# Attention and a two-layer network in one kernel: the first two pairs' k exponentials, the first decode blocks and constant products at the start

## The chip, the cores and the metric

One core of a Trainium2 chip runs the whole program. The metric is the device time of one execution in microseconds, the median of three runs. The trace is of one further execution of the same program.

## The reference

Shapes: batch 8, 8 heads, 576 tokens, head size 64, 128 features; 4608 tokens of 512 values go into a network of 512 to 2048 to 512.

```python
def phi(x):
    proj = np.einsum('bhsd,df->bhsf', x, w_phi)
    proj = proj - np.max(np.abs(proj), axis=-1, keepdims=True)
    return np.concatenate([np.exp(proj), np.exp(-proj)], axis=-1)
q_p, k_p = phi(q), phi(k)
kv = np.einsum('bhsf,bhsd->bhfd', k_p, v)
z = np.sum(k_p, axis=2)
num = np.einsum('bhsf,bhfd->bhsd', q_p, kv)
den = np.einsum('bhsf,bhf->bhs', q_p, z)[..., None] + 1e-06
attn = num / den                      # then heads side by side: x
h = x @ w_in
g = np.maximum(h, 0.0) + alpha * np.minimum(h, 0.0)
return g @ w_out
```

So exp(p - m) and exp(-(p - m)) = exp(-p + m) are wanted for every projected row p, where m is the largest absolute value of the row.

## The kernel before

Attention runs over 32 pairs of heads. A pair's k and q are one DMA (raw), laid with the head size on the partitions, so that one tile of 128 tokens of one head is the weights of a product with w_sb (w_phi), and 128 tokens x 128 features come out in PSUM. project(0) makes the first four tiles of k for both heads (16 product instructions in the trace); project(1) makes the last 64 tokens of k with 64 of q (the two small tiles pl), and then four tiles of q per head. VectorE takes the maximum m of the absolute values (L311) and subtracts it from the PSUM into a tile t in SBUF (L312). k_exp reads t on ScalarE, twice, with scale 1 and -1 (L325, and L320 for the last 64 tokens). q's t is turned by TensorE (q_turn) and its exponentials are taken from PSUM (L402, L404). k_z and k_acc sum and multiply with v on TensorE into the tile kv; kv_out copies it, kv_turn turns it, kv_copy copies it again; num and den are q's products with it.

PSUM: project(0) of the pairs 0 and 1 has a tile of its own per head, from the pool psf (two buffers, tag f); all other projections use one tile pj of both heads (ps_pj, one buffer). So each projection has to wait until the one before it has been read.

The weights of the network come as 64-bit numbers and are decoded in blocks of 256 columns, seven stages each: load (SP), scale (ScalarE), split (four VectorE instructions, L181 to L184), add (GpSimd), high (ScalarE), low (GpSimd), store (SP). Four buffers hold raw blocks.

The order is written out by hand: each step has a due time in units of a pair's slot (places, decode_at), all are sorted, and the engines PE, SP, DVE (VectorE) and Activation (ScalarE) keep that order. GpSimd's order, and the order of all engines in the second pass of the network behind this part, come from the planner of the framework. Pair i has project(0) at i - 0.9955, project(1) at i, k_exp(0) at i - 0.26, k_exp(1) at i + 0.0011, k_z at i + 1.0002, k_acc at i + 1.0012, the turns of kv and q from i + 1.1 on, den at i + 2.0004, num at i + 2.005. Decode block n of the first 20 has its split at 1 + n // 2 + 0.004 for even n and + 0.5 for odd n; its load is due 0.70 earlier, its scale 0.25 earlier, add, high and low 0.15, 0.42 and 0.55 later. "Project i/c" below means project(c) of pair i.

Of the kernel before, what the change touches and what calls it, by code (L numbers as in the profile page):

```python
# [8 lines left out]
F32 = mybir.dt.float32  # L9
F32R = mybir.dt.float32r  # L10
U32 = mybir.dt.uint32
AF = mybir.ActivationFunctionType
ALU = mybir.AluOpType
# [3 lines left out]
P = 128  # L17
B, H, S, D = 8, 8, 576, 64
FD = 128
# [20 lines left out]
WA = (0.0040, 0.50)  # L40
# [3 lines left out]
G_BUFS = 2  # L44
P_BUFS = 2
NV = 5
X_BUFS = 2
RAW_BUFS = 2
N2A = 3
# [59 lines left out]
def fused_kernel(ctx: ExitStack, tc: tile.TileContext, kq, v, w_phi, w_in, w_out, alpha, out):  # L109
# [24 lines left out]
    al = cst.tile([P, NF], F32, name="al")  # L134
# [1 line left out]
    act.dma_start(w_sb, w_phi)  # L136
    act.dma_start(al, alpha)
    aln = cst.tile([P, NF], F32, name="aln")
    dve.tensor_scalar(aln, al, -1.0, None, op0=ALU.mult)

    w1t = ctx.enter_context(tc.tile_pool(name="w1t", bufs=1, side="right"))
    ffn1 = ExitStack()
# [78 lines left out]
    def decode_at(t, blk):  # L221
        return [(t + (WT if t < TL else WL)[k], lambda u=u: u(*blk, WN)) for k, u in stages.items()]
# [38 lines left out]
    ps_pj = att.enter_context(tc.tile_pool(name="ps_pj", bufs=1, space=PSUM))  # L261
    ps_kv = att.enter_context(tc.tile_pool(name="ps_kv", bufs=1, space=PSUM))

    ones = cat.tile([P, 32], F32, name="ones")
    pool.memset(ones, 1.0)
    k4buf = []
# [5 lines left out]
    def attention_units(i):  # L272
        b, hp = divmod(i, NP)
        c = {}
# [8 lines left out]
            nc.sync.dma_start(c["v"], v[i])  # L283

        def project(ch):
            t = c["t", ch] = wk.tile([P, 2, 4 + ch, FD], F32, tag=f"t{ch}", name=f"t{i}_{ch}", bufs=1 + ch)
            dst, out, js = {}, [], [0, 1, 2, 3]
            if ch:
                js = [4] + js
                for h in range(2):  # L290
                    p1 = ps_m.tile([P, 1, 1, FD], F32, tag="m", name=f"pl{i}_{h}")
                    dst[h, 4] = p1[:, 0, 0]
                    out.append((slice(h, h + 1), slice(4, 5), p1))
            if ch == 0 and i < 2:
                for h in range(2):
                    p1 = psf.tile([P, 1, 4, FD], F32, tag="f", name=f"pj{i}_{ch}_{h}")
                    dst.update({(h, j): p1[:, 0, j] for j in range(4)})
                    out.append((slice(h, h + 1), slice(0, 4), p1))
            else:
                p2 = ps_pj.tile([P, 2, 4, FD], F32, tag="pj", name=f"pj{i}_{ch}")  # L300
                dst.update({(h, j): p2[:, h, j] for h in range(2) for j in range(4)})
                out.append((slice(0, 2), slice(0, 4), p2))
            for j in js:
                for h in range(2):
                    hs = slice(h * D, (h + 1) * D)
                    ts = slice((4 * ch + j) * P, (4 * ch + j + 1) * P)
                    pe.matmul(dst[h, j], lhsT=c["raw"][hs, ts], rhs=w_sb[hs], start=True, stop=True)  # L307
            for n, (hs, js, src) in enumerate(out):
                nh, nj = hs.stop - hs.start, js.stop - js.start
                m = wk.tile([P, nh, nj], F32, tag="m", name=f"m{i}_{ch}_{n}", bufs=4)  # L310
                dve.tensor_reduce(m, src, axis=AX.X, op=ALU.max, apply_absolute_value=True)  # L311
                dve.tensor_tensor(  # L312
                    t[:, hs, js], src, m.unsqueeze(3).broadcast_to([P, nh, nj, FD]), op=ALU.subtract
                )

        def k_exp(ch):
            if ch == 1:
                x = k4buf[i % 2]
                for a, sg in enumerate((1.0, -1.0)):
                    act.activation(x[0:64, a], c["t", 1][0:64, :, 0, :], AF.Exp, scale=sg)  # L320
                c["x", ch] = x.rearrange("p a (h n) f -> p a h n f", n=1)
                return
            x = wk.tile([P, 2, 2, 4, FD], F32, tag="x", name=f"xk{i}", bufs=X_BUFS)
            for a, sg in enumerate((1.0, -1.0)):
                act.activation(x[:, a], c["t", 0], AF.Exp, scale=sg)  # L325
            c["x", ch] = x

# [255 lines left out]
    def first_x():  # L583
        st = {}

        def fetch0():
            st["xr"] = xhl.tile([P, NK, C2], F32, tag="xr", name="xr2_0", bufs=XR_BUFS)
            nc.sync.dma_start(st["xr"], x_d[:, :, :C2].rearrange("k p s -> p k s"))
            xs[0] = []

        def cast0(j):
            if j % 2 == 0:
                st["xq"] = qp.tile([P, 2, 2, S], F32R, tag="qf", name=f"x2hl0{j}", bufs=QH_BUFS)
            xh, xl = (st["xq"][:, n, j % 2, :C2] for n in range(2))
            rnd(act, xh, st["xr"][:, j])
            xs[0].append((xh, xl))

        def low0(j):
            xh, xl = xs[0][j]
            low(dve, xl, st["xr"][:, j], xh)  # L600

        us = [(X0T[0], fetch0)]
        for j in range(NK):
            us.append((X0T[1 + j], lambda j=j: cast0(j)))
            us.append((X0T[1 + j] + X0L, lambda j=j: low0(j)))
        return us
# [10 lines left out]
    late += [(ff, z) for z in (1, 0) for ff in range(NF1 + NA, NF - NL)]  # L617
    blocks = [(ff, z, o) for ff, z in late for o in range(0, 512, WN)]
    for n, blk in enumerate(first):
        todo += decode_at(1 + n // 2 + WA[n % 2], blk)  # L620
    for n, blk in enumerate(blocks):
        todo += decode_at(W2A + W2D * n, blk)
    todo += first_x()
    et = mybir.EngineType
    pinned = {et.PE, et.SP, et.DVE, et.Activation}

# [174 lines left out]
```

## Time and profile before

| | us |
|---|---|
| median of 3 runs (1139.42 to 1140.46) | 1140.08 |
| the profiled execution's own time | 1140.04 |
| its span, first to last instruction | 1138.2 |
| PE busy | 1114.4 |
| DVE busy | 634.0 |
| ACT busy | 561.1 |
| POOL busy | 213.9 |

Busy time is summed over the instructions of an engine. Where rows carry a time in us from the start of the span, that is the start of the first instruction of the row, and the second number is the stretch that the row's instructions cover together. PE is TensorE, DVE VectorE, ACT ScalarE, POOL GpSimd, SP the engine that issues most DMAs.

### The profile page before, as it was taken

How to read it: one execution, taken by the hardware profiler on the slowest of the kernel's cores; microseconds unless marked ns; L12 is line 12 of the kernel's file. 1: busy time of each engine (PE TensorE's matmuls, PEld its weight loads, DVE VectorE, ACT ScalarE, POOL GpSimd, SP SyncE). 2: the span in 40 equal slices, each digit the busy share in tenths (PEclk: the TensorE clock that was granted, in tenths of full speed). 3: DMA queues.
4: the chain of work that ended last, by engine and by line, in shares of the span. 5: the costliest groups of instructions: out<-in, count | busy, mean ns of one | idle time of the engine just before them, and what ended most of it. 6: DMA issues, size and time to landing. Idle time of an engine off the chain costs nothing.

```text
span 1138.2 us, 18351 instructions
## 1 busy us (share of the span) xinstructions
PE 1114.4 (98%) x7232; PEld 865.2 (76%) x7232; DVE 634.0 (56%) x978; ACT 561.1 (49%) x1149; POOL 213.9 (19%) x219
## 2 busy tenths in 40 slices
PE   6999999999999999999999999999999999999998
PEld 5766767777777777677778788888888888888886
DVE  7888957798687777836861342424242333333322
ACT  4777656666666765664543333333333333433332
POOL 1345332322424142243542000000000000000000
PEclk9999999999999999999999999999999999999999
DMA  5467264555556365466627030303030302112021
GB/s 190 147 186 219 68 194 143 172 164 183 162 167 195 99 211 167 146 202 219 227 65 246 32 111 1 111 1 111 1 111 1 111 1 75 37 33 79 1 74 37
DMA packets 74101, 133.68 MB, mean 117 GB/s; under 512 B 14624, under 2 KB 24480, under 8 KB 73376
## 3 DMA queue, kind: packets, MB, share of 16 engines
q1 hardware_dynamic: 71712, 122.48, 33.7%
q0 software_dynamic: 2016, 9.96, 2.5%
q8 instruction: 57, 0.93, 0.3%
q14 instruction: 28, 0.23, 0.1%
q10 hardware_dynamic: 288, 0.07, 0.0%
HBM read 93.92 MB, written 38.42 MB: 116 GB/s over the span
## 4 chain that ended last, share of the span: by engine, by line
PE 88%; DVE 6%; DMA 4%; ACT 2%; issue 1%; SPq 0%; DVEq 0%; ACTq 0%
PE h L503 11%; PE h L505 11%; PE h L504 11%; PE po L511 8%; PE po L509 8%; PE po L510 8%; PE kv L348 6%; PE n L413 5%; PE pj L307 5%; PE o L511 3%; PE o L509 3%; PE o L510 3%; PE d L431 2%; PE qt L394 2%; DMA xr<-x_d 2%; PE kv L365 1%
## 5 line engine op out<-in xcount | busy, mean ns | idle before, releaser
L240 DVE SCALAR_TENSOR_TENSOR g<-r,aln,g 128x512 f32<-128x512 f32 x144 | 111.7, 775 | 307.1 <-ACT g L236 306.9
L235 ACT ACTIVATE r<-h 128x512 f32<-128x512 f32 x144 | 86.5, 601 | 293.3 <-PE h L505 293.2
L127 DVE TENSOR_TENSOR gl<-g,gh 128x512 fp32r<-128x512 f32 x144 | 104.7, 727 | 67.6 <-ACT gh L123 67.1
L123 ACT CAST gh<-g 128x512 fp32r<-128x512 f32 x144 | 90.0, 625 | 85.6 <-DVE g L240 85.6
L236 ACT ACTIVATE g<-h 128x512 f32<-128x512 f32 x144 | 86.0, 598 | 1.0 <-DMA part_d<-os 1.0
L509 PE MATMUL po<-gh,wd 128*128 128x512 f32 x216 | 84.6, 392 | 0.7 <-ACT gh L123 0.7
L510 PE MATMUL po<-gh,wd 128*128 128x512 f32 x216 | 84.7, 392 | 0.0
L511 PE MATMUL po<-gl,wd 128*128 128x512 f32 x216 | 84.5, 391 | 0.0
L311 DVE TENSOR_REDUCE m<-pj 128x8 f32<-128x1024 f32 (+1 forms) x66 | 78.2, 1185 | 10.4 <-PE pj L307 10.3
L307 PE MATMUL pj<-w_sb,raw 64*128 64x128 f32 x1024 | 73.2, 283 | 9.8 <-DMA w_sb<-w_phi_dram 4.6
L307 PEld LDWEIGHTS pj<-w_sb,raw 64*128 64x128 f32 x1024 | 64.1, 192 | 23.3 <-issue 15.6
L189 POOL TENSOR_TENSOR aw<-ew,aw 128x256 f32<-128x256 f32 x64 | 56.6, 885 | 128.6 <-DVE ew L184 128.6
L312 DVE TENSOR_TENSOR t<-pj,m 128x1024 f32<-128x1024 f32 (+1 forms) x66 | 78.7, 1192 | 2.3
L509 PE MATMUL o<-gh,w 128*128 128x512 f32 x180 | 76.0, 422 | 2.6 <-ACT os L554 2.4
L463 POOL TENSOR_TENSOR s<-s,rr 128x576 f32<-128x576 f32 x32 | 48.5, 1517 | 145.3 <-DMA rr<-rec_d 127.7
L503 PE MATMUL h<-xh,w 128*128 128x512 f32 x180 | 75.8, 421 | 0.0
L511 PE MATMUL o<-gl,w 128*128 128x512 f32 x180 | 71.7, 399 | 3.6 <-DVE gl L127 3.4
L404 ACT ACTIVATE qf<-qt 128x512 f32<-128x512 f32 x128 | 68.4, 615 | 6.3 <-PE qt L394 6.3
L511 PE MATMUL po<-gl,w 128*128 128x512 f32 x180 | 69.7, 390 | 1.4 <-DVE gl L127 1.4
L505 PE MATMUL h<-xl,w 128*128 128x512 f32 x180 | 70.7, 393 | 0.0
L510 PE MATMUL o<-gh,w 128*128 128x512 f32 x180 | 70.6, 392 | 0.0
L504 PE MATMUL h<-xh,w 128*128 128x512 f32 x180 | 70.5, 392 | 0.0
(105 smaller groups left out, 2402.6 us busy)
## 6 DMA issues: line engine op xcount, KB each, us to landing
xr<-x_d SPq DMA_DIRECT2D x18, 1024.0 KB
raw<-kq_dram SPq DMA_DIRECT2D x31, 576.0 KB
v<-v_dram SPq DMA_DIRECT2D x32, 320.0 KB
w_d<-raww SPq DMA_DIRECT2D x38, 256.0 KB
rr<-rec_d SPq DMA_DIRECT2D x64, 144.0 KB
x_d<-s SPq DMA_DIRECT2D x32, 288.0 KB
part_d<-os SPq DMA_DIRECT2D x36, 256.0 KB
pt<-part_d SPq DMA_DIRECT2D x9, 1024.0 KB
```

Source lines behind the costliest of these rows:

```text
L123: return act.copy(dst, src)
L127: return eng.tensor_tensor(dst, src, f(hi), op=ALU.subtract)
L235: act.activation(st["r"], ps, AF.Relu, scale=-1.0)
L236: act.activation(st["g"], ps, AF.Relu)
L240: dve.scalar_tensor_tensor(g, st["r"], aln[:, ff : ff + 1], g, op0=ALU.mult, op1=ALU.add)
L307: pe.matmul(dst[h, j], lhsT=c["raw"][hs, ts], rhs=w_sb[hs], start=True, stop=True)
L503: pe.matmul(ps, lhsT=wt[0][:, ws], rhs=xh, start=n == 0, stop=False)
L504: pe.matmul(ps, lhsT=wt[1][:, ws], rhs=xh, start=False, stop=False)
L505: pe.matmul(ps, lhsT=wt[0][:, ws], rhs=xl, start=False, stop=n == NK - 1)
L509: pe.matmul(ps, lhsT=wt[2][:, ws], rhs=gh, start=first, stop=False)
L510: pe.matmul(ps, lhsT=wt[3][:, ws], rhs=gh, start=False, stop=False)
L511: pe.matmul(ps, lhsT=wt[2][:, ws], rhs=gl, start=False, stop=last)
```

## The change

Four edits, all at the start of the kernel:

- Pairs 0 and 1 (i < NX): project(0) no longer subtracts the maximum on VectorE and has no tile t. VectorE makes the negative of the maximum in a small tile mn; ScalarE takes the exponentials from PSUM, one instruction per head, sign and tile of 128 tokens (16 per pair), with mn or m as bias.
- Decode blocks 0 and 1 have their splits due at 2.25 and 2.75 instead of 1.004 and 1.5; all their other stages move with them.
- A tile of ones (warm), set by VectorE, is multiplied by itself seven times (NWARM) into the PSUM tile that kv uses later, ahead of all other products; one exponential of it goes to ScalarE.
- The negative of alpha (aln) is made at due time 1.5 instead of first of all on VectorE.

```diff
@@ -44,6 +44,8 @@
 G_BUFS = 2
 P_BUFS = 2
 NV = 5
+NX = 2
+NWARM = 7
 X_BUFS = 2
 RAW_BUFS = 2
 N2A = 3
@@ -136,7 +138,6 @@
     act.dma_start(w_sb, w_phi)
     act.dma_start(al, alpha)
     aln = cst.tile([P, NF], F32, name="aln")
-    dve.tensor_scalar(aln, al, -1.0, None, op0=ALU.mult)
 
     w1t = ctx.enter_context(tc.tile_pool(name="w1t", bufs=1, side="right"))
     ffn1 = ExitStack()
@@ -261,6 +262,14 @@
     ps_pj = att.enter_context(tc.tile_pool(name="ps_pj", bufs=1, space=PSUM))
     ps_kv = att.enter_context(tc.tile_pool(name="ps_kv", bufs=1, space=PSUM))
 
+    warm = cat.tile([P, P], F32, name="warm")
+    dve.memset(warm, 1.0)
+    warm_e = cat.tile([P, 1], F32, name="warm_e")
+    act.activation(warm_e, warm[:, 0:1], AF.Exp)
+    ps_w = ps_kv.tile([P, 3, FD], F32, tag="kv", name="warm_up")
+    for n in range(NWARM):
+        pe.matmul(ps_w[:, 0], lhsT=warm, rhs=warm, start=True, stop=True)
+
     ones = cat.tile([P, 32], F32, name="ones")
     pool.memset(ones, 1.0)
     k4buf = []
@@ -283,7 +292,8 @@
             nc.sync.dma_start(c["v"], v[i])
 
         def project(ch):
-            t = c["t", ch] = wk.tile([P, 2, 4 + ch, FD], F32, tag=f"t{ch}", name=f"t{i}_{ch}", bufs=1 + ch)
+            if ch or i >= NX:
+                t = c["t", ch] = wk.tile([P, 2, 4 + ch, FD], F32, tag=f"t{ch}", name=f"t{i}_{ch}", bufs=1 + ch)
             dst, out, js = {}, [], [0, 1, 2, 3]
             if ch:
                 js = [4] + js
@@ -291,7 +301,7 @@
                     p1 = ps_m.tile([P, 1, 1, FD], F32, tag="m", name=f"pl{i}_{h}")
                     dst[h, 4] = p1[:, 0, 0]
                     out.append((slice(h, h + 1), slice(4, 5), p1))
-            if ch == 0 and i < 2:
+            if ch == 0 and i < NX:
                 for h in range(2):
                     p1 = psf.tile([P, 1, 4, FD], F32, tag="f", name=f"pj{i}_{ch}_{h}")
                     dst.update({(h, j): p1[:, 0, j] for j in range(4)})
@@ -309,6 +319,11 @@
                 nh, nj = hs.stop - hs.start, js.stop - js.start
                 m = wk.tile([P, nh, nj], F32, tag="m", name=f"m{i}_{ch}_{n}", bufs=4)
                 dve.tensor_reduce(m, src, axis=AX.X, op=ALU.max, apply_absolute_value=True)
+                if ch == 0 and i < NX:
+                    mn = wk.tile([P, nh, nj], F32, tag="mn", name=f"mn{i}_{n}", bufs=4)
+                    dve.tensor_scalar(mn, m, -1.0, None, op0=ALU.mult)
+                    c["pm", hs.start] = src[:, 0], m, mn
+                    continue
                 dve.tensor_tensor(
                     t[:, hs, js], src, m.unsqueeze(3).broadcast_to([P, nh, nj, FD]), op=ALU.subtract
                 )
@@ -321,7 +336,12 @@
                 c["x", ch] = x.rearrange("p a (h n) f -> p a h n f", n=1)
                 return
             x = wk.tile([P, 2, 2, 4, FD], F32, tag="x", name=f"xk{i}", bufs=X_BUFS)
-            for a, sg in enumerate((1.0, -1.0)):
+            for h in range(2) if i < NX else ():
+                src, m, mn = c["pm", h]
+                for a, (sg, bias) in enumerate(((1.0, mn), (-1.0, m))):
+                    for j in range(4):
+                        act.activation(x[:, a, h, j], src[:, j], AF.Exp, scale=sg, bias=bias[:, 0, j : j + 1])
+            for a, sg in enumerate((1.0, -1.0) if i >= NX else ()):
                 act.activation(x[:, a], c["t", 0], AF.Exp, scale=sg)
             c["x", ch] = x
 
@@ -617,10 +637,11 @@
     late += [(ff, z) for z in (1, 0) for ff in range(NF1 + NA, NF - NL)]
     blocks = [(ff, z, o) for ff, z in late for o in range(0, 512, WN)]
     for n, blk in enumerate(first):
-        todo += decode_at(1 + n // 2 + WA[n % 2], blk)
+        todo += decode_at(2.25 + 0.5 * n if n < 2 else 1 + n // 2 + WA[n % 2], blk)
     for n, blk in enumerate(blocks):
         todo += decode_at(W2A + W2D * n, blk)
     todo += first_x()
+    todo.append((1.5, lambda: dve.tensor_scalar(aln, al, -1.0, None, op0=ALU.mult)))
     et = mybir.EngineType
     pinned = {et.PE, et.SP, et.DVE, et.Activation}
 
```

## Rows read from the trace of the kernel before

**Rows 1.** The page's busy time, share of the span and instructions of each engine.
```profile
PE 1114.4 (98%) x7232; PEld 865.2 (76%) x7232; DVE 634.0 (56%) x978; ACT 561.1 (49%) x1149; POOL 213.9 (19%) x219
```

**Rows 2.** Busy time by stretch: stretch, length, each engine's busy us, granted clock, DMA.
```profile
0.00:10.00 10.00, 4.66 (x45) 4.50 (x47) 3.38 (x8) 1.82 (x2) 1.75 (x9) 1.00 0.51 166
10.00:20.00 10.00, 6.51 (x107) 5.02 (x104) 9.61 (x17) 5.46 (x10) 0.00 (x0) 1.00 0.83 279
20.00:30.00 10.00, 9.40 (x135) 6.88 (x133) 9.28 (x19) 7.52 (x18) 3.39 (x5) 1.00 0.37 127
30.00:40.00 10.00, 10.00 (x141) 7.12 (x137) 8.55 (x16) 8.14 (x19) 2.46 (x4) 1.00 0.08 26
```

**Rows 3.** TensorE's waits in 0 to 60 us: total, times, longest.
```profile
PE pj L307 <- DVE t L312: 3.5, 3, 2.1
```

**Rows 4.** Order of time, w_sb's load and TensorE's projections: start, us, instruction, idle before.
```profile
0.75 0.41 ACTq L136 DMA_DIRECT2D w_sb<-w_phi_dram  x1
...
4.57 2.08 PE L307 MATMUL pj<-w_sb,raw 64*128 64x128 f32 x16 [4.57 <-DMA w_sb<-w_phi_dram]
...
9.57 1.02 PE L307 MATMUL pj<-w_sb,raw 64*128 64x128 f32 x13 [0.77 <-DVE t L312]
...
19.12 1.16 PE L307 MATMUL pj<-w_sb,raw 64*128 64x128 f32 x16 [1.41 <-issue]
...
22.91 1.16 PE L307 MATMUL pj<-w_sb,raw 64*128 64x128 f32 x16 [0.60 <-DVE t L312]
...
28.51 1.16 PE L307 MATMUL pj<-w_sb,raw 64*128 64x128 f32 x16
...
39.09 1.16 PE L307 MATMUL pj<-w_sb,raw 64*128 64x128 f32 x16
```

**Rows 5.** Line 307 on TensorE in two stretches: ns least/median/most, first and last start.
```profile
L307 PE MATMUL pj<-w_sb,raw x10: 417/417/419, 4.9 to 5.8; 64*128 64x128 f32 x10
...
L307 PE MATMUL pj<-w_sb,raw x4: 271/272/272, 8.3 to 8.5; 64*128 64x128 f32 x4
```

**Rows 6.** Order of time, VectorE from 6 to 23 us, eight of its instructions.
```profile
6.69 0.69 DVE L311 TENSOR_REDUCE m<-pj 128x4 f32<-128x512 f32 x1 [1.09 <-PE pj L307]
...
9.34 0.28 DVE L311 TENSOR_REDUCE m<-pl 128x1 f32<-128x128 f32 x1
...
11.64 1.22 DVE L312 TENSOR_TENSOR t<-pj,m 128x1024 f32<-128x1024 f32 x1
12.78 0.68 DVE L311 TENSOR_REDUCE m<-pj 128x4 f32<-128x512 f32 x1
...
17.79 1.22 DVE L312 TENSOR_TENSOR t<-pj,m 128x1024 f32<-128x1024 f32 x1
18.93 0.28 DVE L181 TENSOR_SCALAR aw<-aw 128x256 uint32<-128x256 uint32 x1
...
20.38 1.22 DVE L311 TENSOR_REDUCE m<-pj 128x8 f32<-128x1024 f32 x1
...
21.63 1.23 DVE L312 TENSOR_TENSOR t<-pj,m 128x1024 f32<-128x1024 f32 x1
```

**Rows 7.** Small instructions: aln and k's exponentials in order of time; L402 in all.
```profile
5.42 0.17 DVE L139 TENSOR_SCALAR aln<-al 128x16 f32<-128x16 f32 x1 [5.42 <-DMA al<-alpha_dram]
...
9.46 2.00 ACT L325 ACTIVATE xk<-t 128x1024 f32<-128x1024 f32 x2 [6.51 <-DVE t L312]
...
21.55 0.44 ACT L402 ACTIVATE qf<-qt 128x128 f32<-128x128 f32 x2
...
L402 ACT ACTIVATE qf<-qt x64: 261/277/313, 21.6 to 503.0; 128x128 f32<-128x128 f32 x64
```

**Rows 8.** Order of time, VectorE in the slot from 28.51 to 39.09.
```profile
30.98 1.22 DVE L312 TENSOR_TENSOR t<-pj,m 128x1024 f32<-128x1024 f32 x1
...
33.21 0.29 DVE L181 TENSOR_SCALAR aw<-aw 128x256 uint32<-128x256 uint32 x1 [1.00 <-ACT aw L173]
...
35.08 0.28 DVE L311 TENSOR_REDUCE m<-pl 128x1 f32<-128x128 f32 x1
...
37.38 1.22 DVE L312 TENSOR_TENSOR t<-pj,m 128x1024 f32<-128x1024 f32 x1
```

## The prediction

> **What bounds the kernel now.** I read the share of busy time first, then the first 40 us cut into tens, then the waits of TensorE, and last the order of instructions there. TensorE is busy for 98% of the span [rows 1], so outside the beginning little can be won by anything that isn't fewer products. The beginning is the exception: in the first 10 us TensorE is busy for 4.66, in the second for 6.51, in the third for 9.40, and in the fourth for all of it [rows 2]. 4.57 us of what is missing is the wait for the first data, w_sb, issued at 0.75 [rows 4]; no edit touches that. After it about 4.9 us are idle (0.77 + 3.49 + 0.60, from the same slices), and 3.5 of these are put down to VectorE's subtraction t (L312) [rows 3]. So the whole prize is those 4.9 us, and what the first products lose by being slow: the first 16 need 2.08 us, later 16 need 1.16 [rows 4], because one takes 417 ns at first and 272 ns from about 8.3 us on [rows 5]. By the ratio this is TensorE's clock at its lower and at its upper level (1.2 and 2.4 GHz); it rose after TensorE had worked since 4.57. The granted clock reads 1.00 in all slices [rows 2] and doesn't show it; the durations do.
>
> The order to see is a ring: project (PE) fills PSUM, VectorE reduces and subtracts, and only the end of the subtraction gives the PSUM back to the next project. From 6.69 to 22.86 VectorE goes from one instruction to the next, with the four of a decode split near 19 among them [rows 6]; project 1/0 waits for it at 9.57, project 2/0 at 19.12, project 2/1 at 22.91 [rows 4]. From 28.51 to 39.09 one slot (pair) takes 10.58 us and TensorE is full [rows 2, 4].
>
> **The change part by part.** I follow the ring once, with each time worked out from durations of before.
>
> Step 1, constant products. Seven 128x128 products should run between about 1 us and the landing at 4.57; w_sb is not moved. If the clock is up by then, the first 16 products last 1.16 instead of 2.08, and VectorE's first reduction starts at 5.77 instead of 6.69: 0.92 earlier. If it isn't, nothing is gained. They cost nothing as long as they end before 4.57: by 14 product instructions at the 0.13 us apart that the first 16 took (2.08/16) [rows 4] they take 1.8 us, and even at twice that 3.7, which still ends near 4.6. Moving aln is free: it waited for its own load until 5.42 and lasts 0.17 [rows 7], and the memset takes its place.
>
> Step 2, VectorE loses four subtractions of 0.69 us (two per pair, the length of the reduction before them [rows 6], with one subtraction of twice the size at 1.22) and gains four tiny negations, for which the nearest row is aln, 0.17 us [rows 7]. I take 0.15, since the next instruction overlaps the end of the last. Net: 1.38 - 0.30 = 1.08 us less per pair.
>
> Step 3, ScalarE. Two exponentials of 1.0 us [rows 7] become 16 of 128x128 from PSUM, each with a bias of its own per row. No row has such a bias. The nearest is q's exponential of the same shape without it, L402: 277 ns each [rows 7], of which two stand in 0.44 us, so that the next starts 0.167 after the first. That is the lower bound of one step; the upper is no overlap, 0.277. I take 0.25, nearer the upper end, because the instruction has an operand more than the row. 16 of them are 4.0 us instead of 2.0. The Trainium skill, "ScalarE: Activation LUTs", section "What ACT_TABLE_LOAD costs", says that a bias read per partition adds about 93 ns; no run here shows it yet. By that page the step would be an estimated 0.26, and the sum below would be 0.16 us worse.
>
> Now the ring. Reductions of pair 0 at 5.77 and 6.6, negations done at 6.6 and 7.45. ScalarE starts at 6.65, and both halves are through at 6.65 + 16 x 0.25 = 10.65. The two PSUM tiles are now held by ScalarE, where VectorE let go of them at 9.4. VectorE goes on meanwhile: project 0/1 from 9.34 to 12.86 took 3.52 [rows 6], so 7.45 + 3.52 = 10.97. Project 1/0 needs the second tile: its 13 remaining products (1.02 us [rows 4]) run from about 10.8 to 11.8. Its reduction starts at 11.85 instead of 12.78 [rows 6]. From there to the end of project 1/1's subtraction before took 19.01 - 12.78 = 6.23 [rows 6]; less 1.08 it ends at 17.0, instead of 19.01. TensorE is free by then: project 1/1, k's sums and products fill 11.8 to 16.9 by their lengths of before. Project 2/0 therefore runs from 17.1. In the kernel before, decode block 0's split stood in front of its reduction (18.93 to 20.47, reduction at 20.38 [rows 6]). The split is gone from there, but project 2/0 began at 19.12, so the reduction could not have come before 20.33 anyway: that removal alone brings nothing. Now the reduction comes at 18.3, its subtraction ends at 20.8 instead of 22.86, and project 2/1 starts at 20.9 instead of 22.91. k's second set of 16 exponentials (12.7 to 16.7) and the copy behind it are done by 18.3, so the turns of pair 0 stand before project 2/1 as they did. **The gain at this point is 2.0 us**, and project 3/0 would start at 26.5 instead of 28.51.
>
> With 0.167 per step ScalarE is no longer last, VectorE is (10.97), and the gain is 2.8; with 0.277 it is 1.55. Without the clock each ScalarE-bound value is 0.92 lower.
>
> Step 4, the two blocks of decode that were moved. Their DMA issues go from the crowded stretch of 10 to 20 us [rows 2] to SP places at 1.55 and 2.05; four raw buffers hold them, so SP doesn't stop for them, and I cost that at nothing. Their splits, though, go into the slot that TensorE already fills. In order of due times VectorE now has three splits (blocks 0, 3 and 1; 2.25, 2.5, 2.75) between project 3/0 and project 3/1, where it had one. Before: project 3/0 starts at T = 28.51, its subtraction ends 3.69 later (30.98 + 1.22), VectorE then idles for 1.0 until the split at 33.21, goes on to project 3/1 at 35.08 and ends its subtraction at 38.60 (37.38 + 1.22), 3.52 after that [rows 8]. TensorE starts project 4/0 at T + 10.58 [rows 4], 0.5 after that. Behind the wait stand num of pair 1 and all later work, since TensorE keeps its order. Now: 3.69 + three splits + 3.52 + 0.1. A split, start to next start, took 1.45 (18.93 to 20.38 [rows 6]) to 1.87 (33.21 to 35.08 [rows 8]); at 1.65 the sum is T + 12.26. So **TensorE waits for 1.7 us before project 4/0** (1.1 to 2.3 by the bounds). VectorE catches up in the following slots, which have some 1 us of slack, and no second stall of this kind follows. ScalarE's four added operations in that slot lie within this same wait.
>
> Sum: 2.0 - 1.7 = 0.3 us gained. Against the profiled execution, 1140.04 (span 1138.2 and 1.84 around it; the median is 1140.08): 1139.75, say **1139.8 us**. All later work is chained to TensorE, and shifts with it. Bounds of the forecast: 1138.3 (2.8 - 1.1) to 1140.8 (1.55 - 2.3).
>
> **The rivals.**
> A: the gain is kept. It needs that the three splits don't hold project 4/0, for instance because VectorE is ahead of TensorE there. Against it: VectorE is idle for only 1.0 us in that slot [rows 8] and gets 3.3 more. For it: the 1.0 of idle time and a quick split leave 1.1. Without the stall the time is 1140.04 - 2.0 = 1138.0, and at the short ScalarE step 1137.2.
> B, slower: the constant products don't raise the clock for the first data, and ScalarE, holding the two PSUM tiles, becomes the ring's bound. TensorE is idle again between the last of them and 4.57, and nothing before shows how the clock stands then. The gain falls to 1.1 at 0.25 per exponential, to 0.6 at 0.277; less 1.7 the time is 1140.6 to 1141.1, and with the long splits 1141.7. It decides as soon as the clock stays down; with the clock up, from 0.27 us per exponential. The Trainium skill, "TensorE: Matmul & The Clock Gate", section "Part 1: The HAM clock gate", says that the slow state is the default and work releases it, at a moment that differs from run to run; our rows agree as far as the rise near 8 us goes [rows 5].
> C: the change does what it says, but the planner, which orders GpSimd everywhere and all engines in the last part, comes to another order, because its own clock is changed at the start. TensorE's waits outside the beginning are small, so I price this at 2 to 4 us to either side: 1136 to 1144.
>
> **How the numbers follow.** Forecast 0.55, A 0.15, B 0.18, C 0.12. A difference under 0.2% (2.3 us) can't be told from no change in a measurement of this kernel; so "faster" is under 1137.8 and "slower" over 1142.4. The forecast and B lie wholly within. A gives about half of its chance to faster, C two fifths to either side and the rest within: faster 0.13, same 0.81, slower 0.06. The range takes in the forecast, B, and most of A: 1137.6 to 1141.7.
>
> **What would show it.** First products of 272 ns at 4.57 and a first reduction near 5.8 show step 1; steps of 0.25 us on ScalarE between 6.65 and 10.7 show step 3; project 2/1 near 20.9 shows the gain; a wait of TensorE of 1 to 2 us for VectorE's subtraction near 37, before project 4/0, shows step 4. If project 4/0 starts before 37.5, A is right; if it starts after 39.1, B. If both kernels agree at 60 us and differ in the end, it is C.

## The result, and the profile after

| | before | after |
|---|---|---|
| median of 13 runs each, us | 1140.08 | 1145.13 |
| range of the runs | 1138.58 to 1144.02 | 1141.45 to 1149.77 |
| ratio | | 1.0042, 95% interval 1.0025 to 1.0058 |
| the profiled execution's own time | 1140.04 | 1141.45 |
| its span | 1138.2 | 1139.5 |

The change makes the kernel 0.42% slower, outside the forecast range and not "within 0.2%". The profiled execution of after is the fastest of its 13 runs; so its trace shows less than the median loses, and a second trace was taken (e10 below). The mean granted clock of after's runs lies between 0.993 and 0.998 (0.9958 in the mean of 13); the kernel before has 0.9978 in the mean of the 96 runs beside the experiments. One run of e6 below, 1248.97 us at a granted clock of 0.851, is left out of all that is worked out from e6's runs.

The page of after answers [rows 1]. TensorE is as full as before:

```profile
PE 1117.4 (98%) x7246; PEld 868.6 (76%) x7246; DVE 635.0 (56%) x979; ACT 565.2 (50%) x1178; POOL 215.1 (19%) x219
```

The ring in order of time (as [rows 4], [rows 6], [rows 7]): start, us, engine, line, instruction, idle before.

```profile
1.07 3.36 PE L271 MATMUL warm_up<-warm 128*128 128x128 f32 x14 [1.07 <-DVE warm L266]
...
4.36 1.67 PE L317 MATMUL pj<-w_sb,raw 64*128 64x128 f32 x16
...
6.07 0.69 DVE L321 TENSOR_REDUCE m<-pj 128x4 f32<-128x512 f32 x1 [5.05 <-PE pj L317]
6.79 0.17 DVE L324 TENSOR_SCALAR mn<-m 128x4 f32<-128x4 f32 x1
...
7.06 1.14 ACT L343 ACTIVATE xk<-pj,mn 128x128 f32<-128x128 f32 x4 [3.89 <-DVE mn L324]
...
9.28 0.48 PE L317 MATMUL pj<-w_sb,raw 64*128 64x128 f32 x2 [2.13 <-ACT xk L343]
...
10.07 1.22 ACT L343 ACTIVATE xk<-pj,m 128x128 f32<-128x128 f32 x4
...
11.34 1.04 PE L317 MATMUL pj<-w_sb,raw 64*128 64x128 f32 x13 [1.57 <-ACT xk L343]
...
12.33 0.69 DVE L321 TENSOR_REDUCE m<-pj 128x4 f32<-128x512 f32 x1 [1.14 <-PE pj L317]
...
12.60 2.11 PE L317 MATMUL pj<-w_sb,raw 64*128 64x128 f32 x15
...
16.25 1.22 DVE L327 TENSOR_TENSOR t<-pj,m 128x1024 f32<-128x1024 f32 x1
...
18.67 1.16 PE L317 MATMUL pj<-w_sb,raw 64*128 64x128 f32 x16
...
22.42 1.16 PE L317 MATMUL pj<-w_sb,raw 64*128 64x128 f32 x16 [0.59 <-DVE t L327]
...
28.02 1.16 PE L317 MATMUL pj<-w_sb,raw 64*128 64x128 f32 x16
```

The last three are project 2/0, 2/1 and 3/0, forecast at 17.1, 20.9 and 26.5. Up to 12 us the order is the forecast one, some 0.5 us late: ScalarE's exponentials start 0.25 us apart (8 from 7.06 to 9.07, 16 ending at 11.29), and project 1/0 waits for them. What is new is project 1/1: 15 products take 2.11 us where 16 took 1.16 in the kernel before:

```profile
13.01 1.16 PE L307 MATMUL pj<-w_sb,raw 64*128 64x128 f32 x16 [2.08 <-DVE t L312]
```

The stretches of 1 us of after show why (length, busy us of PE, PEld, DVE, ACT, POOL, then the granted clock, DMA share, GB/s):

```profile
7.00:8.00 1.00, 0.15 (x4) 0.00 (x0) 0.93 (x4) 0.94 (x4) 0.00 (x0) 1.00 0.00 0
8.00:9.00 1.00, 0.00 (x0) 0.00 (x0) 0.97 (x4) 1.00 (x5) 0.00 (x0) 1.00 0.84 281
...
10.00:11.00 1.00, 0.00 (x0) 0.00 (x0) 1.00 (x1) 1.00 (x6) 0.00 (x0) 1.00 0.74 293
11.00:12.00 1.00, 0.66 (x10) 0.66 (x12) 0.19 (x1) 0.95 (x4) 0.00 (x0) 1.00 0.05 18
12.00:13.00 1.00, 1.00 (x16) 1.00 (x14) 0.67 (x1) 0.00 (x0) 0.00 (x0) 0.65 0.00 0
13.00:14.00 1.00, 1.00 (x14) 1.00 (x11) 0.93 (x5) 0.68 (x3) 0.00 (x0) 0.50 0.08 16
14.00:15.00 1.00, 1.00 (x14) 0.76 (x15) 0.93 (x5) 1.00 (x5) 0.00 (x0) 0.50 0.00 0
15.00:16.00 1.00, 1.00 (x32) 0.94 (x28) 1.00 (x2) 1.00 (x5) 0.00 (x0) 0.65 0.33 69
```

From 7.15 to 11.34 TensorE is busy for 0.48 us, and then its clock falls from the upper level (2.4 GHz) to the lower (1.2) for most of four slices: 0.35 + 0.50 + 0.50 + 0.35 = 1.7 us of full-speed work are lost. The kernel before has waits of 0.77 and 2.08 us there, and this trace of it shows no fall.

The second place is the slot of [rows 8], in order of time, with GpSimd and TensorE:

```profile
30.49 1.22 DVE L327 TENSOR_TENSOR t<-pj,m 128x1024 f32<-128x1024 f32 x1
...
31.63 0.28 DVE L182 TENSOR_SCALAR aw<-aw 128x256 uint32<-128x256 uint32 x1
...
33.07 0.29 DVE L182 TENSOR_SCALAR aw<-aw 128x256 uint32<-128x256 uint32 x1
...
33.31 0.73 POOL L129 TENSOR_TENSOR w<-aw,w 128x256 fp32r<-128x256 f32 x1 [4.94 <-ACT w L125]
33.40 0.92 DVE L183 SCALAR_TENSOR_TENSOR aw<-raww,aw 128x256 uint32<-128x256 uint32 x1
34.00 0.92 POOL L190 TENSOR_TENSOR aw<-ew,aw 128x256 f32<-128x256 f32 x1
...
35.45 0.29 DVE L182 TENSOR_SCALAR aw<-aw 128x256 uint32<-128x256 uint32 x1
...
37.75 0.28 DVE L321 TENSOR_REDUCE m<-pl 128x1 f32<-128x128 f32 x1
...
40.05 1.23 DVE L327 TENSOR_TENSOR t<-pj,m 128x1024 f32<-128x1024 f32 x1
...
41.38 1.16 PE L317 MATMUL pj<-w_sb,raw 64*128 64x128 f32 x16 [2.71 <-issue]
```

The three splits stand at 31.63, 33.07 and 35.45 and end with the next reduction at 37.75: 1.44, 2.38 and 2.30 us. TensorE waits 2.71 us for the subtraction that ends at 41.28. In this run no fall of the clock follows, and project 4/0 is 2.3 us later than before.

### The profile page after: what moved, and what is told of

It is laid out like the page before. It is cut to its first block, busy times and chain, and to the rows that moved or that the text cites. A ratio compares the mean times of both kernels' runs of the same rounds, so it can differ in the third digit from the quotient of the medians.

```text
span 1139.5 us, 18406 instructions
## 1 busy us (share of the span) xinstructions
PE 1117.4 (98%) x7246; PEld 868.6 (76%) x7246; DVE 635.0 (56%) x979; ACT 565.2 (50%) x1178; POOL 215.1 (19%) x219
## 4 chain that ended last, share of the span: by engine, by line
PE 89%; DMA 5%; DVE 3%; ACT 1%; issue 1%; POOL 0%; SPq 0%; ACTq 0%; POOLq 0%; DVEq 0%
PE h L523 11%; PE h L525 11%; PE h L524 11%; PE po L531 8%; PE po L529 8%; PE po L530 8%; PE kv L368 6%; PE pj L317 5%; PE n L433 5%; PE o L531 3%; PE o L529 3%; PE o L530 3%; PE d L451 3%; PE qt L414 2%; DMA xr<-x_d 2%; PE kv L385 2%
## 5 line engine op out<-in xcount | busy, mean ns | idle before, releaser
L327 DVE TENSOR_TENSOR t<-pj,m 128x1024 f32<-128x1024 f32 x62 | 75.9, 1225 | 2.1
```

## The experiments

Theory S: the three splits hold project 4/0, and that is the loss. Theory C: TensorE's clock falls behind its waits, and that is the loss. Medians stand beside those of the kernel before on the same chips: 1140.42 for e1 to e4, 1140.73 for e5 to e7, 1140.34 for e8 to e11, 1140.11 for e12 to e14.

| | edit | median us | ratio, 95% interval | project 3/0 | project 4/0 | lost to the clock |
|---|---|---|---|---|---|---|
| before | | | | 28.51 | 39.09 | 2.5 |
| after | | 1145.13 | 1.0025 to 1.0058 | 28.02 | 41.38 | 4.7 |
| e1 | decode moved | 1145.48 | 1.0029 to 1.0059 | 28.06 | 41.41 | 3.8 |
| e2 | constant products | 1141.11 | 0.9997 to 1.0023 | 27.98 | 38.56 | 3.5 |
| e3 | exponentials | 1142.24 | 1.0004 to 1.0023 | 30.76 | 41.34 | 3.2 |
| e4 | products, exponentials | 1142.25 | 1.0005 to 1.0025 | 29.51 | 40.09 | 4.9 |
| e5 | e4, products in the ring | 1140.90 | 0.9993 to 1.0016 | 27.25 | 37.83 | 1.9 |
| e6 | after, products in the ring | 1147.81 | 1.0046 to 1.0078 | 26.52 | 39.86 | 3.7 |
| e7 | decode block 0 alone moved | 1142.24 | 0.9998 to 1.0019 | 29.41 | 40.45 | 2.5 |
| e8 | e6, products before 4/0 | 1140.24 | 0.999 to 1.0017 | 27.40 | 40.86 | 1.0 |
| e9 | e5, products near 147 us | 1140.05 | 0.9985 to 1.0008 | 26.59 | 37.16 | 1.0 |
| e10 | after again, one run | 1146.52 | | 29.16 | 42.52 | 8.0 |
| e11 | before again, one run | 1140.90 | | 28.30 | 38.88 | 1.1 |
| e12 | e1, products before 4/0 | 1147.73 | 1.0046 to 1.0072 | 28.09 | 41.54 | 5.3 |
| e13 | e2, products in the ring | 1142.66 | 1.0011 to 1.0031 | 28.29 | 38.87 | 2.5 |
| e14 | e5, products near 165 us | 1142.83 | 1.0009 to 1.003 | 27.22 | 37.80 | 1.4 |

The project columns are starts in us in the one trace of each kernel. The last column is worked out from the granted clock in the mean of a kernel's runs, as (1 - clock) x its span; so it is full-speed work lost at most, since TensorE may also stand still in that time. It also misses the slow first products, where the granted clock reads 1.00 [rows 5].

**The parts alone.** e1, e2, e3 and e4 take parts of the change back. e1 keeps only this:

```diff
-        todo += decode_at(1 + n // 2 + WA[n % 2], blk)
+        todo += decode_at(2.25 + 0.5 * n if n < 2 else 1 + n // 2 + WA[n % 2], blk)
```

The other three have this line as before. e2 keeps the constant products and the moved aln, e3 the exponentials from PSUM, e4 both.

> The kernel before with the two decode blocks moved and nothing else. Theory S (the three splits in one slot hold project 4/0): a wait of TensorE of 2 to 3 us near 38 us and some 2 us more in all, 1141.5 to 1143, at a granted clock as before. Theory C (the loss is TensorE's clock, which falls when the ring leaves TensorE idle after an early warm start): no warm start, so the clock stays at 1.000 in the mean as before, and at most 1 us is lost, under 1141.5.

> The kernel before with the constant products (and aln moved) and nothing else. Theory S: 0.9 us faster at the start and no loss, about 1139.2. Theory C: TensorE is at full clock from about 5 us, then idle for 1 to 2 us at a time while VectorE subtracts; the granted clock falls to 0.5 for about 3 us between 10 and 20 us, and the 0.9 is lost again or more: 1140 to 1143, mean clock 0.996 to 0.999, spread of several us between runs.

> The kernel before with the 16 exponentials per pair from PSUM and nothing else; decode and start as before. Theory S: about 1.0 us gained in the ring by the measured 0.25 us per exponential, no wait near 38 us: about 1139. Theory C: the first products are slow as before, the clock rises near 8 us; then TensorE idles for 1.5 us twice while ScalarE holds the PSUM tiles. If these gaps alone make the clock fall, the mean is under 1.000 and the time 1140 to 1142; if the early rise is needed too, it is 1139.

> The changed kernel with the two decode blocks back in their old places. Theory S: no wait near 38 us, so 2.7 us less than the changed kernel in each run: 1138.5 at its best, 1142.5 in the median. Theory C: the clock falls near 12 us as in the changed kernel, and the spread of several us between runs stays; 1141 to 1145 in the median.

e1 loses as much as the whole change, which no other part does: theory S named the part, but its 1141.5 to 1143 was too little. Before's mean clock, put at 1.000 there, is 0.9977 in its 29 runs beside e1. The trace of e1 has more than the wait. Project 4/0 in TensorE's order of time:

```profile
41.41 2.08 PE L310 MATMUL pj<-w_sb,raw 64*128 64x128 f32 x16 [2.70 <-issue]
```

The stretches of 1 us from there, columns as above:

```profile
41.00:42.00 1.00, 0.59 (x5) 0.62 (x7) 0.97 (x4) 0.65 (x3) 0.00 (x0) 0.54 0.00 0
42.00:43.00 1.00, 1.00 (x12) 1.00 (x12) 0.76 (x3) 0.43 (x2) 0.03 (x1) 0.50 0.39 23
43.00:44.00 1.00, 1.00 (x10) 0.53 (x8) 0.47 (x1) 0.00 (x0) 0.69 (x1) 0.50 0.40 37
```

The wait is that of the changed kernel, and here the clock falls behind it: project 4/0 takes 2.08 us, and project 5/0 starts at 54.36 instead of 49.66. So behind the same wait project 5/0 is 2.3 us later than before in after's first trace and 4.7 here. For theory C, e2's gain of 0.5 us at project 4/0 isn't there in the median, 1141.11, which lies in theory C's range and not at 1139.2; e3's 1142.24 is over both its expectations, and in it the clock falls near 12 us, beside ScalarE's waits of 2.39 and 1.57, and project 3/0 comes 2.2 us late. But e1 and e2 have TensorE's waits of before in the ring (0.91 and 2.08 us), and both traces show a fall there too, at 13.8 and 12.4 us. So ScalarE's longer waits aren't needed for it. e4, without the moved decode, still has 6.8 us of half clock (10.7 to 17.5). Its median, 1142.25, fits both expectations (1142.5, and 1141 to 1145) and doesn't decide between them. Without the moved decode, then, the change costs about 1.8 us, with it 5.

**The clock held up.** e5 and e6 add products to TensorE's idle stretches, in e4 and in the changed kernel; project 1/0 makes one head after the other, so that there is a place between them (e8, e9 and e14 have the same two edits):

```diff
+            if split and h == 1 and j == js[0]:
+                fill(6)
...
+            if i == 0 and ch == 1:
+                fill(8)
```

> e4 with 14 more constant products in TensorE's two long waits near 7 to 11 us: eight behind project 0/1, six between the two heads of project 1/0, which are now made one after the other. Theory C (the fall of the clock after these waits is the loss of e4): no stretch at 0.5 between 9 and 20 us, project 3/0 near 26.5 us instead of 28 to 30, 2 us less than e4: 1140.0 in the median. Rival (the clock's fall there is hidden, since ScalarE and VectorE set the ring): granted clock 1.00 there, but the same 1142.

> The changed kernel with the same 14 products. Theory C: 2 us less than the changed kernel, 1143 in the median, since the wait before project 4/0 stays (2.7 us). Theory S alone: no difference, 1145.

Three of e6's groups of products, in order of time:

```profile
20.92 1.16 PE L322 MATMUL pj<-w_sb,raw 64*128 64x128 f32 x16 [0.59 <-DVE t L334]
26.52 1.16 PE L322 MATMUL pj<-w_sb,raw 64*128 64x128 f32 x16
...
39.86 1.16 PE L322 MATMUL pj<-w_sb,raw 64*128 64x128 f32 x16 [2.70 <-issue]
```

And a stretch of 1 us:

```profile
13.00:14.00 1.00, 1.00 (x26) 0.88 (x26) 0.93 (x4) 1.00 (x6) 0.00 (x0) 1.00 0.00 0
```

VectorE's first reduction of pair 1:

```profile
10.63 0.68 DVE L328 TENSOR_REDUCE m<-pj 128x4 f32<-128x512 f32 x1
```

With products in the waits the clock stays at 1.00, and project 2/1 and 3/0 come at 20.92 and 26.52: 2.0 us ahead of before and within 0.02 us of the forecast. That the match is so close is partly luck, since the order of project 1/0 isn't the forecast one: VectorE reduces the first head of pair 1 at 10.63, in after at 12.33, and ScalarE goes on to pair 1 at 11.61 instead of 13.32. No run has the products without this order.

What the fall alone costs is read from after's own rows: VectorE's subtraction for project 1/1 ends at 17.47 (16.25 + 1.22), and project 2/0 could have followed at about 17.6; TensorE, with its slow products, gets to it at 18.67. So the fall takes 1.1 us of the 1.5 that are missing at project 2/1; the rest had been lost by 12.33, where VectorE is 0.5 us late. What the rows show, then, is that the gain was there and that the fall took most of it. How early the clock rises counts too: in the five traces with these edits the first 16 products of data take from 1.20 us (e6) to 2.08 (e8), and project 3/0 comes at 26.52 (e6) to 27.40 (e8).

e5's median lies 0.2 us over the kernel before on the same chip, where e4's lay 1.8 over it: 1.7 us less, near the 2 expected. e6's median, 1147.81 instead of the 1143 expected, lies 7.1 us over the kernel before, after's 5.05: the 2 us gained before 30 us don't show in it, so something behind the wait at 38 us outweighs them.

e7 is e1 with one block only, so that two splits stand in the slot:

```diff
-        todo += decode_at(1 + n // 2 + WA[n % 2], blk)
+        todo += decode_at(2.25 if n < 1 else 1 + n // 2 + WA[n % 2], blk)
```

> The kernel before with only block 0 of the decode moved (to 2.25), so that two splits instead of three stand between project 3/0 and project 3/1. Theory S: by the 2.04 us that a split took in the changed kernel's slot (three in 6.12), the wait before project 4/0 is 2.7 - 2.0 = 0.7 us, and the time 1141 in the median. Rival (the moved loads and ScalarE's work cost, not the number of splits): half of the loss of e1 or more, 1143.

Project 4/0 came 11.04 us after project 3/0 instead of 10.58: a wait of 0.46, near the 0.7 expected of the number of splits. The median, 1142.24, is in between, and its interval takes in no change at all; its trace also has a fall in the ring, from 11.5 to 18.3 us.

**The wait, and what follows it.** e8 fills the wait before project 4/0 in e6, and e12 does the same in e1, with the same constant tile, none of its products ahead of the data, and aln moved as in the change:

```diff
+            if ch == 0 and i == 4:
+                w4 = psf.tile([P, FD], F32, tag="f", name="warm_four")
+                for _ in range(12):
+                    pe.matmul(w4, lhsT=warm, rhs=warm, start=True, stop=True)
```

> e6 with twelve more constant products just ahead of project 4/0, in the wait that the three splits make. The wait stays (2.7 us less the 2.6 us that the products fill at full speed), so project 4/0 starts no earlier. Theory C+S (the wait costs its length, and in many runs a fall of the clock behind it besides): the granted clock doesn't fall between 38 and 55 us, and the median is 1 to 2 us under e6, 1146 or less. Rival (the length of the wait is all that it costs): the same median as e6, 1147 to 1148.

> The changed kernel as it is, for a second trace, since its first is of the fastest of 13 runs (1141.45 against a median of 1145.1). Theory C+S: project 4/0 starts 2 us or more later than in the kernel before, and there is more than one stretch at half clock: one in the ring and one behind the wait at 38 us or a later wait; 1143 to 1148. Rival (something else differs from run to run): one fall as in the first trace, and the time lost elsewhere.

> The kernel before as it is, for a second trace, since its first shows no fall of the clock between 5 and 1130 us. Theory C: its waits of 2 us at 11 to 13 us and at 80 to 100 us can bring a fall too, in some runs; by the clocks of its runs (0.996 to 0.999) one fall of some 3.4 us is usual: 1139 to 1142.

> e1 (the two decode blocks moved, nothing else) with twelve constant products ahead of project 4/0, in the wait made by the splits. If the fall of the clock behind the wait is half of e1's loss: no fall between 40 and 55 us, 2 to 3 us under e1, 1143 in the median, and what is left against the kernel before is the wait, 2 to 3 us. If the wait alone is the loss: 1145.5 as e1.

e10, the changed kernel's second trace, is 1.4 us above its median; TensorE in order of time:

```profile
42.52 1.16 PE L317 MATMUL pj<-w_sb,raw 64*128 64x128 f32 x16 [2.71 <-issue]
43.61 3.71 PE L433 MATMUL n<-qf,sf 128*64 128x288 f32 x16
...
55.67 1.16 PE L317 MATMUL pj<-w_sb,raw 64*128 64x128 f32 x16 [0.87 <-PE kv L368]
```

And stretches of 1 us:

```profile
44.00:45.00 1.00, 1.00 (x8) 0.53 (x6) 1.00 (x1) 0.00 (x0) 0.72 (x1) 0.53 0.55 51
45.00:46.00 1.00, 1.00 (x6) 0.49 (x4) 0.97 (x2) 0.40 (x1) 0.00 (x0) 0.50 0.86 313
46.00:47.00 1.00, 1.00 (x6) 0.24 (x2) 0.32 (x1) 0.00 (x0) 0.00 (x0) 0.50 1.05 350
47.00:48.00 1.00, 1.00 (x8) 0.76 (x7) 0.00 (x0) 0.48 (x2) 0.00 (x0) 0.76 0.97 166
```

Against the first trace of before, project 3/0 is late by 0.65 us (a longer fall in the ring, to 17 us), project 4/0 by 3.4, project 5/0 by 6.0 (55.67 - 49.66), and the last products by 6.2. By 56 us the 6.0 are the ring's lost gain, the wait, and the fall behind the wait. But they aren't simply carried to the end: the distance shrinks in steps, near 88, 98, 150 and 250 us, 3.5 are left at 620, and a wait of 2.26 us near 633 with a fall behind it (634.6 to 638.0) brings 2.7 again. In after's first trace it likewise goes from 2.3 at 56 us to 0.4 at 400 and 1.2 at the end. e11, the second trace of before, has one fall, near 153 us, and none in the ring; there the clock isn't up before 16.2 us. Project 1/1 and project 2/1 in it:

```profile
12.67 2.08 PE L307 MATMUL pj<-w_sb,raw 64*128 64x128 f32 x16 [0.96 <-DVE t L312]
...
22.70 1.16 PE L307 MATMUL pj<-w_sb,raw 64*128 64x128 f32 x16 [0.59 <-DVE t L312]
```

Project 2/1 comes at 22.70 all the same, 0.2 earlier than in the first trace, with the first data 0.3 earlier: in the ring of before VectorE sets the pace, and slow products fit into TensorE's waits.

e8's wait is full of products, in order of time:

```profile
37.98 2.94 PE L310 MATMUL warm_four<-warm 128*128 128x128 f32 x24
40.86 1.16 PE L326 MATMUL pj<-w_sb,raw 64*128 64x128 f32 x16
```

No fall follows:

```profile
43.00:48.00 5.00, 5.00 (x83) 4.07 (x83) 3.61 (x9) 4.17 (x12) 0.04 (x1) 1.00 0.70 230
```

Project 4/0 starts no earlier against project 3/0 (13.46 us behind it), and the median is 1140.24, 7.6 us under e6 and that of the kernel before. That is far more than the 1 to 2 expected of one fall. e12 says not to read it as the price of that fall alone: there too the wait is filled and the clock stays at 1.00 from 40 to 55 us, project 5/0 starts at 52.11 instead of e1's 54.36, but the median is 1147.73, 4.7 over what was expected. Its trace falls later, behind a wait that the change doesn't touch, here in order of time:

```profile
155.99 0.80 PE L530 MATMUL o<-gh,w 128*128 128x512 f32 x1 [3.51 <-ACT os L575]
```

The stretches behind it:

```profile
155.00:158.00 3.00, 2.01 (x5) 1.63 (x6) 0.21 (x1) 3.00 (x6) 2.42 (x2) 0.64 0.38 128
158.00:161.00 3.00, 3.00 (x17) 2.21 (x17) 0.02 (x1) 2.32 (x4) 1.35 (x2) 0.79 0.69 241
```

There is one fall more in the ring, at 12.5 us, again with the waits of before, and one near 637 us. So what the early part gains or loses is not all kept: it also shifts when TensorE comes to later waits. e6's trace is of the fastest of its five runs, e12's of the slowest of its five.

**Later waits, and a better version.** e9 and e14 put eight products near the wait of 150 us into e5, e9 with this due time and e14 with 35 in the place of 30:

```diff
+    def fill_late():
+        w5 = ps_m.tile([P, FD], F32, tag="m", name="warm_late")
+        for _ in range(8):
+            pe.matmul(w5, lhsT=warm, rhs=warm, start=True, stop=True)
+
+    todo.append((F0 + FR * 30 / 40 - 0.0001, fill_late))
```

e13 is e2 with products in its two waits of the ring:

```diff
+            if i == 1 and ch == 1:
+                fill(8)
...
+            if i == 0 and ch == 1:
+                fill(4)
```

> e5 with eight more constant products ahead of the network's third output tile, near 150 us, where TensorE waits for 1.5 to 2.4 us for ScalarE's copy (os) in every trace so far. Theory C: a fall of the clock behind that wait (as in the traces of e3, e6 and e7) can't come any more, 0.5 to 1 us less than e5 in the median: 1140.2, a little under the kernel before. Rival (falls there are rare in timed runs): 1140.9 as e5.

> e2 (constant products at the start) with 4 more behind project 0/1 and 8 more ahead of project 1/1, where TensorE waits for VectorE; k's exponentials and decode as in the kernel before. If ScalarE's exponentials from PSUM bring something once the clock is held up, this is slower than e5 by 0.7 to 1.5 us: project 3/0 near 27.7 us instead of 26.6 to 27.3. If they bring nothing, both are alike.

> e5 with eight more constant products ahead of the fourth output tile of the network's first block, where the wait of 1.5 to 2.4 us for ScalarE's copy really stands (e9's stood one tile too early, and the wait stayed). No fall of the clock near 150 us, and no cost, since the products take 1.8 us: 0.5 to 1 us under the kernel before, 1139.5.

In e9 the products stood where the wait is (147.13 to 149.08), but the wait went on for 1.87 us behind them and the clock fell: the whole of it is set by the load xr<-x_d, for which ScalarE's copy has to wait, and TensorE had come 2.8 us early. By 157 us 0.1 of these 2.8 were left. So its median, 1140.05, is near the 1140.2 expected by luck: neither the wait nor the fall was gone. The expectation of e14 misread this as a wrong place; its own products came at 165 us, behind the wait, which was 3.23 us with a fall. e14 therefore says nothing on filling that wait.

Its median, 3.3 over the 1139.5 expected and 1.9 over e5 with the same start to 0.03 us (2.55 when each is set against the kernel before on its own chip), shows how much the later waits vary. e13's project 3/0, 28.29 where 27.7 was expected, is that of before: without ScalarE's exponentials the clock held up brings 0.2 us; with them, and the other order of project 1/0, it brings 1.1 to 2.0 us (e8, e5, e14, e9, e6). e13's median is 2.55 us over the kernel before. No version beat the kernel before: e9 is at 0.9997 (0.9985 to 1.0008), e8 within 0.999 to 1.0017.

**The clock over all runs.** The last column of the table counts what no single trace can. After loses 4.7 us to the lower clock where before loses 2.5: 2.2 of the 5.05 us. The rest, 2.8, is near the wait of 2.71, as if nothing of the ring's gain were left; this is a difference of sums and doesn't show where the time is lost. e4 is 1.8 us slower than before and loses 2.4 more to the clock, so the rest of it gains 0.6. With products in the waits the clock's part comes down to 1.0 to 1.9 in e5, e8, e9 and e14, less than before's own, but the medians only reach before's or stay over it (e14); in e13 and e6, which have such products too, it is 2.5 and 3.7. That other waits take what the clock gives back there is likely and not shown. In e6 and e12 the clock explains 1.2 and 2.7 of 7.1 and 7.6 us; the rest, 5.9 and 4.9, is more than their one wait.

## Why the prediction was wrong

**Step 1, constant products.** They ended at 4.43 and the first data products started at 4.36: free, as said, and within the 1.8 to 3.7 us reckoned (3.36). The clock was up for all of the first data in none of the ten traces with them: the first 16 took 1.20 us in e6, 1.67 in after, and 2.08 in e4, e8, e10 and e13, as without them [rows 4]. So the 0.92 of this step came in part or not at all. The sum counted it whole; rival B had that as a chance.

**Step 2 and 3, VectorE and ScalarE.** The negation took 0.17 us (0.15 assumed). The exponentials took 0.25 us from one to the next, as assumed; one lasts 396 ns in the median with mn and 430 with m, against 277 without a bias [rows 7]. The first of the two:

```profile
L343 ACT ACTIVATE xk<-pj,mn x16: 359/396/442, 7.1 to 16.1; 128x128 f32<-128x128 f32 x16
```

The estimate of 0.26 that the prediction worked out from the Trainium skill ("ScalarE: Activation LUTs", section "What ACT_TABLE_LOAD costs") agrees with the 0.25 of a step; the 119 to 153 ns by which one instruction is longer are more than the 93 of that page.

**The ring.** This is the first step that failed. The sum put the ring's products at their full-speed lengths ("by their lengths of before") although the same sum kept TensorE idle from about 7 to 10.8 us for ScalarE, and it left 0.1 us between the end of the products (16.9) and that of the subtraction (17.0). In after the clock fell, and TensorE came to project 2/0 1.1 us behind the subtraction, which itself was 0.5 late; the gain of 2.0 at project 2/1 became 0.5. In e10, e4 and e3, where the lower clock lasts 6.8 us, it became a loss of 0.65 to 2.25. The clock fell there in every trace of a kernel with any part of the change and without products in the ring (after, e10, e1, e2, e3, e4, e7, e12); of the two of before one has no fall, and in the other the clock rose only at 16.2 us. In e1, e2 and e12, where VectorE still subtracts for the first two pairs, the fall costs little: from the first data to project 3/0 it is 24.09 us in e1 and 24.06 in e12, 23.94 in the first trace of before. So the waits and the steps of ScalarE were forecast nearly right, and what was left out is the clock, which waits in the ring can take away. The Trainium skill, "TensorE: Matmul & The Clock Gate", section "HAM oscillation — how this bites in real kernels", tells of a kernel whose waits for data bring the clock down again each time; a rival drawn from it would have come true here, at shorter waits (2.13 and 1.57 us in after) than that kernel's. Here a wait of 2.08 us had a fall beside it in e1, e2 and e7, and none in the first trace of before, so the length of that wait alone doesn't decide.

**Step 4, the splits.** The place and the waiting instruction were right; the wait was 2.71 instead of 1.7, outside its bounds of 1.1 to 2.3. The term that was mis-sized is the split, 2.04 us in the mean instead of 1.65: the first took 1.44, the second and third 2.38 and 2.30. In those two L183 takes 0.92 and 0.86 where it took 0.42 in the first, L184 takes 0.65 where it took 0.29, and GpSimd's own steps of the decode (33.31 to 34.92, and again from 35.61 to 37.22) run beside them. The prediction took its upper bound from one split with one GpSimd step beside it and didn't count that two more blocks bring two more adds and lows into the slot. The traces of e1, e6, e7 and e8 have the same in this slot: these two instructions are long where a GpSimd step runs beside them and short where none does (in e1 and e7 they are L184 and L185). That GpSimd's steps are the cause is read from this overlap and wasn't tried alone. e7, with two splits, had a wait of 0.46.

**After step 4.** "No second stall of this kind follows" was wrong in the way that costs most: behind the wait the clock falls in e1 and e10 (not in after's first trace or e6's), for some 2.5 us more. "All later work is chained to TensorE, and shifts with it" held from 56 to 88 us in every trace, and not at the later waits, above all near 150 us, where e9's gain was lost and a fall came in either kernel (e11, e9), and near 630 us (e10, e12). The prediction called TensorE's waits outside the beginning small; from 40 us to its last product it stands idle for 10.4 us in the trace of before, more than the 4.9 that were to be won, and with 2.44 us in one piece near 150 us.

**Rivals.** A (gain kept) needs no wait before 4/0 and is refuted by the 2.70 to 2.71 us in all four traces with three splits and no products there. B has the right side and half of the mechanism, but holds the clock's fall to the first data and 1.7 us at most. C (another order of the rest) didn't come: in the first traces every engine, GpSimd too, has the same instructions in the same order in after as in before from 47.1 us on.

**What stays open.** How the medians of e6 and e12 come to lie 7.5 us above e8's. At 60 us e6's trace is ahead of e8's by 1.0 us; the waits and falls near 150 and 630 us differ from run to run, and one trace of each doesn't say how often they come. So the part of the change that costs is shown (the moved decode, e1), and so is the wait that it makes; how that wait of 2.7 us becomes 5 us in the median is shown for one run near the median (e10) and not in general. It is also open what decides whether a wait of some 2 us brings the clock down.

## What to carry to other kernels

A term in a sum for TensorE has a speed, and each wait that a change makes or lengthens puts it at risk: price a wait like the 2.7 us here as the wait and, as a chance of its own, the products behind it at half clock (1.7 us of work here). What such a fall costs in time depends on who sets the pace there: 1.1 us in after's ring, 0.1 to 0.2 in e1's and e12's, where TensorE waits for VectorE anyway. Work moved into a slot is priced with all its engines, since here VectorE's steps were up to 0.5 us longer where GpSimd's steps of the same work ran beside them. When one profiled run is the best of many, its trace explains the best run; take a second before the median is explained.

## What the runs showed of the hardware

- One fall of TensorE's clock costs about 1.7 us of full-speed work (0.35 + 0.50 + 0.50 + 0.35 in after), and twice that where it lasts twice as long (e4). It came behind a stretch of 4.2 us with 0.48 us of work (after), at the end of a wait of 2.70 (e1) and of one of 3.51 (e12), and not at a wait of 2.71 in after; near waits of 2.08 it came in e1, e2 and e7 and not in the first trace of before.
- Products of a constant tile in such a stretch hold the clock at 1.00: 14 of them in the ring (e6), 12 in the wait before project 4/0 (e8, e12). Eight of them at the start of a wait that went on for 1.87 us didn't (e9).
- The granted clock reads 1.00 at the start in every trace, yet the first products of data take 417 ns instead of 272 [rows 5] in all but e6 and e9; in e11 this lasts to 16.2 us.
